# A retention layer and a low-rank mixer on one core: the prologue in another order

## The chip, the core and the metric

The kernel runs on one core of one Trainium2 chip. The metric is the time of one execution on the device in microseconds. The kernel before takes 223.32 us (median of 4 runs, 223.24 to 223.55). Engines are named as in the profile: PE is TensorE (PEld its weight loads), DVE is VectorE, ACT is ScalarE, POOL is GpSimd, SP is SyncE, which issues transfers.

## What is computed

The inputs q, k and v have 4 batches, 8 heads, 768 positions and 64 columns. A recurrent retention with one decay per head gives x with 512 columns per position; a low-rank mixing over positions (U: 768x32, V: 32x768) is added to x; an MLP (512 to 2048 and back, relu) is added to that.

```python
state = gamma * state + k_t outer v_t            # per batch and head, 64x64
y_t   = scale * q_t @ state
x     = y as [batch, 768, 512]
u     = x + (x^T @ U @ V)^T
out   = u + relu(u @ w_ch1) @ w_ch2
```

## The kernel before, in words

The recurrence is done in chunks: inside a chunk, scores of k against q are masked and multiplied with v; what came earlier enters as a state matrix. The decays are multiplied into q and k beforehand.

Batch 0 is the prologue. It is done in three blocks `sc` = 0, 1, 2 of 256 positions. For each block `prep_block` scales or casts the loaded halves of k, q and v (engine "P" is GpSimd, "D" VectorE, "A" ScalarE; `prep_pair` does both halves); `turn_block` transposes k or q on TensorE, with a copy from PSUM by the engines in its string; `score_block` makes scores of one parity and masks them (where its engine is "A", ScalarE copies to `a_raw` and GpSimd applies the mask); `state_half` adds half a block's outer products to the state bank and ScalarE copies the state; `mix_block` multiplies state by q and scores by v into two PSUM banks, which are copied to `xs[0]`. `keep_busy` issues matmuls whose result nobody reads. The loop at line 858 writes this out for all three blocks, one block's mix standing in the next block's round.

After the loop GpSimd casts w_ch1 (`prep_w1`), the last block is mixed, `spread_v` and `spread_u` lay V and U out with selection matmuls, `x_turn` transposes x into four PSUM banks, `lr_proj` multiplies x by U, line 909 adds V times that to the transposed x, and the copies of those banks are the input of batch 0's MLP (line 755).

From there on `weave` interleaves the MLP pieces of one batch with the attention of the next, at marks given as shares of the MLP's length. Each engine runs its instructions in program order. `prep_keys` scales k and q of batch 1 on GpSimd (line 306), `turn_pe` turns them on TensorE (line 465).

Loads are issued on SP's queue in one fixed list: batch 0's k, q, v by block, then U and V, w_ch1, the first four loads of batch 1, w_ch2, the rest of batch 1. Sixteen are issued at the start; after that `feed_one` issues one each time a loaded buffer has been taken, into a ring of 16 buffers. PSUM banks come from rings by tag; "mlp" is a ring of three.

Of the kernel before, what the change touches and what calls it, by code (L numbers as in the profile page):

```python
# [10 lines left out]
bf16 = mybir.dt.bfloat16  # L11
fp16 = mybir.dt.float16
AF = mybir.ActivationFunctionType
ALU = mybir.AluOpType
# [4 lines left out]
def kernel(  # L19
# [11 lines left out]
    nc = tc.nc  # L31
    P = 128
    B, H, S, D = q.shape
# [38 lines left out]
    def bank(tag, dtype=fp32):  # L72
        n_bank[0] += 1
        ring = RINGS[tag]
        ring.append(ring.pop(0))
        return psum.tile([P, 2048 // (4 if dtype == fp32 else 2)], dtype,
                         tag=f"bank{ring[-1]}", name=f"{tag}_{n_bank[0]}",
                         bufs=1)
# [4 lines left out]
    def evac(eng, dst, src):  # L83
        if eng == "A":
            nc.scalar.activation(dst, src, AF.Copy)  # L85
        else:
            nc.vector.tensor_copy(out=dst, in_=src)
# [49 lines left out]
    def feed_one(hold=True):  # L137
        if n_fed[0] == len(feed):
            return
        if hold and feed[n_fed[0]][0][:2] == ("k", 3):  # L140
            return
        key, src = feed[n_fed[0]]
        n_fed[0] += 1
        if key[0] == "uv":
            nc.sync.dma_start(
                out=Uf.rearrange("p s two r -> p s (two r)"),
                in_=moe_U.rearrange("(s p two) r -> p s (two r)", p=P, two=2))
            nc.sync.dma_start(
                out=Vf, in_=moe_V.rearrange("r (f t) -> (r f) t", f=NSC))
            return  # L150
        t = rin.tile([P, 512], fp32, tag="in", name=f"in_{n_fed[0]}")
        ready[key] = t
        if key[0] in "qkv":
            t = t.rearrange("p (h d) -> p h d", h=H if len(key) == 3 else 4)
        nc.sync.dma_start(out=t, in_=src)
# [28 lines left out]
    def keep_busy(n, fresh=False, wide=False):  # L184
        if fresh:
            idle_bank[0] = bank("mlp")
        if wide:
            for i in range(n):
                nc.tensor.matmul(idle_bank[0], ones[:, :P], ones, start=True,
                                 stop=True, skip_group_check=True)  # L190
            return
        for i in range(4 * n):
            nc.tensor.matmul(idle_bank[0][:, ts(i % 4, P)], ones[:, :P],  # L193
                             ones[:, :P], start=True, stop=True,
                             skip_group_check=True)
# [110 lines left out]
                nc.gpsimd.tensor_tensor(t, src, g, op=ALU.mult)  # L306
            feed_one()

    def prep_uv():
        take("uv")  # L310
        nc.gpsimd.tensor_copy(out=Uh, in_=Uf)
        nc.gpsimd.tensor_copy(out=Vh, in_=Vf)
        feed_one()

    def spread_u():
        u_p = bank("mlp")
# [6 lines left out]
        return u_p  # L323

    def hold_u(u_p):
        evac("A", Ub.rearrange("p (s x) r -> p x s r", x=2),
             u_p[:, :NCK * RK].rearrange("p (x s r) -> p x s r", x=2, s=NSC))

    def spread_v():
# [21 lines left out]
    live = {}  # L351
    n_state = [0]

    def turn_block(nm, sc, eng):
        src = pre[nm, sc]
        t = blk.tile([P, 4, 2, P], bf16, tag=nm + "T0",
                      name=f"{nm}T0_{sc}")
        np_ = 4 // len(eng)
        for g in range(len(eng)):
            tp = bank("mlp", bf16)  # L360
            for p in range(np_):
                for par in range(2):
                    nc.tensor.transpose(
                        tp[:, ds(2 * P * p, 2 * P)].rearrange(
                            "p (x two m) -> p two x m", x=2, two=2)[:, par],
                        src[:, par, ds(2 * (np_ * g + p), 2)], ident)
            o, i = (t[:, ds(np_ * g, np_)].rearrange("p n x m -> p (n x) m"),
                    tp[:, :2 * P * np_].rearrange("p (n m) -> p n m", m=P))
            if nm == "q":
                o = o.rearrange("p n (m two) -> p n two m", two=2)  # L370
                i = i.rearrange("p n (two m) -> p n two m", two=2)
            evac(eng[g], o, i)
        live[nm, sc] = t

    def state_half(sc, x):

        kd, vb = pre["k", sc], pre["v", sc]
        first = sc == 0 and x == 0
        if first:
            live["st_p"] = bank("st")  # L380
            live["st", 0, 0] = None
        st_p = live["st_p"]
        r = ds(HP * x, HP)
        for par in range(2):
            for p in range(4):
                nc.tensor.matmul(st_p[:, ts(p, P)], kd[r, par, ds(2 * p, 2)],  # L386
                                 vb[r, par, ds(2 * p, 2)],
                                 start=(first and par == 0 and p == 0),
                                 stop=True, skip_group_check=True)
        ns = states[n_state[0] % NST]  # L390
        n_state[0] += 1
        for i in range(2):
            ri = ds(D * i, D)
            evac("A", ns[ri, :, ri], four(st_p)[ri, :, ri])
        live["st", sc + x, 1 - x] = ns
# [22 lines left out]
                nc.gpsimd.tensor_tensor(a, t, m, op=ALU.mult)  # L418
            live["a", sc, par, i] = a

    def mix_block(sc, engs, tags=("o", "qk")):
        if sc == 0:
            xs[0] = xp.tile([P, NCK, DM], fp16, tag="x", name="x_0")
        qT, vb = live.pop(("q", sc)), pre["v", sc]
        o_p = [bank(t) for t in tags]
        for x in range(2):
            st = live.pop(("st", sc, x))
            if st is not None:
                for p in range(4):
                    nc.tensor.matmul(o_p[x][:, ts(p, P)], qT[:, p, x], st[:, p],  # L430
                                     start=(p == 0), stop=False,
                                     skip_group_check=True)
        for par in range(2):
            for h in range(H):
                for x in range(2):
                    r = ds(HP * x, HP)
                    nc.tensor.matmul(
                        o_p[x][:, ts(h, D)],
                        live["a", sc, par, h % 2][r, h // 2], vb[r, par, h],
                        start=(sc == 0 and x == 0 and par == 0 and h == 0),  # L440
                        stop=True, skip_group_check=True)
        for x in range(2):
            evac(engs[x], xs[0][:, 2 * sc + x], o_p[x])

    def turned(nm, b, sc):
        if (nm, b, sc) not in live:
# [90 lines left out]
        uTs[b] = xp.tile([P, NCK, NCB, P], fp16, tag="uT", bufs=1,  # L539
                         name=f"uT_{b}")  # L540

    def lr_proj(b):
        p_p = bank("o" if b else "s")
        for j in range(NCK):
            for c in range(NCB):
                nc.tensor.matmul(p_p[ds(RK * c, RK), :P], Ub[:, j],
                                 xs[b][:, j, ts(c, P)], start=(j == 0),
                                 stop=(j == NCK - 1))
        pcs[b] = rmid.tile([P, P], fp16, tag="pc", name=f"pc_{b}")
        evac("D", pcs[b], p_p[:, :P])  # L550

# [296 lines left out]
    def prep_pair(nm, sc, engs):  # L848
        for hh in range(2):
            prep_block(engs[hh], nm, sc, hh)  # L850
# [4 lines left out]
            nc.vector.tensor_scalar(u_sel[:, x, two], udiff,  # L855
                                    float(two - P * x), None, op0=ALU.is_equal)
    prep_pair("q", 0, "PD")
    for sc in range(NSC):
        last = sc + 1 == NSC
        keep_busy(3 if sc else 9, fresh=not last, wide=not sc)  # L860
        turn_block("k", sc, "D")
        keep_busy(0 if sc else 7, wide=True)
        turn_block("q", sc, "AD" if last else "A")
        prep_pair("v", sc, "PD" if last else "PA")
        if sc:
            state_half(sc - 1, 1)
        else:
            keep_busy(4)
        score_block(sc, 0)
        if last:  # L870
            prep_uv()
        else:
            prep_pair("k", sc + 1, "PD")
            prep_block("P", "q", sc + 1, 0)
            keep_busy(0 if sc else 3)
        if sc:
            score_block(sc, 1, "mlp", "DA")
        else:
            score_block(sc, 1)
        if last:  # L880
            u_p = spread_u()
            state_half(sc, 0)
            hold_u(u_p)
            mix_block(sc - 1, "AD")
            continue
        prep_block("D", "q", sc + 1, 1)
        if sc:
            mix_block(sc - 1, "AA")
        keep_busy(4 if sc else 1, fresh=sc > 0)
        state_half(sc, 0)  # L890
        if sc == 0:
            nc.vector.tensor_scalar(mask, jmat, srange, None, op0=ALU.is_ge)
    for mb in range(4):
        prep_w1(mb)
    mix_block(NSC - 1, "AD", ("s", "s"))
    spread_v()
    x_turn(0, 0)
    x_turn(0, 2)
    block_stack.close()
    gtp = ctx.enter_context(tc.tile_pool(name="gtp", bufs=1))  # L900
    outp = ctx.enter_context(tc.tile_pool(name="outp", bufs=6))
    lr_open(0)
    lr_proj(0)
    for c in range(1, NCB):
        x_turn(c, 0)
        x_turn(c, 2)
    idle_bank[0] = bank("s")
# [129 lines left out]
```

## Time and profile before

| what | value |
|---|---|
| median of 4 runs | 223.32 us |
| the profiled execution | 223.55 us, its span 221.8 us |
| TensorE busy | 213.4 us, 96% of the span |
| VectorE, ScalarE, GpSimd busy | 144.3, 91.2, 83.5 us |
| batch 0's MLP begins (first L755) | 28.13 us |
| batch 1's second q is turned (L465) | 57.42 and 58.42 us |
| read from HBM, written | 27.46 MB, 6.29 MB |

The profile is one execution; its times count from the start of the span. The page gives busy time per engine, 40 slices of the span, DMA queues, and the chain of work that ended last. Other views used are the timeline of one engine (start, length, engine, line, operation, in brackets the idle time before it and who ended it), the waits, and the chain in order of time. A row with x4 or x16 is that many instructions in a run. TensorE's matmuls overlap, so lengths of single rows add up to more than the time they take.

### The profile page before, as it was taken

To read this page: it belongs to the slowest core of one execution; us is meant where nothing else is said; L and a number is where in the kernel's file an instruction comes from. 1 tells how busy PE (TensorE), PEld (TensorE's weight loads), DVE (VectorE), ACT (ScalarE), POOL (GpSimd) and SP (SyncE) were. 2 spreads that over 40 slices of the span, in tenths; PEclk is the share of its full clock that TensorE was granted. 3 is DMA by queue.
4 is the path that set the end of the run, shared out by engine and by line. 5 is a ranking of instruction groups with operands and counts; after the bars stand their busy time and mean duration, and the time that the engine had idled before them with its cause. 6 is when DMAs were issued, how large, how long until landed. Compare 5 with 4: busy or idle time off the path is not lost.

```text
span 221.8 us, 5520 instructions
## 1 busy us (share of the span) xinstructions
PE 213.4 (96%) x2235; PEld 147.7 (67%) x2235; DVE 144.3 (65%) x306; ACT 91.2 (41%) x187; POOL 83.5 (38%) x121
## 2 busy tenths in 40 slices
PE   7879999999899999999999999999999999999994
PEld 2668854595455555666778884756788856668884
DVE  7578656225474567698897756498868542867543
ACT  3357654474556223775712005666420035551000
POOL 5467777887978868000099900000000000000000
PEclk9999999999999999999999999999999999999999
DMA  5998999999999999999999597900000961000043
GB/s 167 302 292 239 271 354 255 339 386 225 239 239 232 243 207 233 162 317 257 218 228 214 142 179 193 141 0 3 1 3 33 148 218 29 4 0 0 7 162 118
DMA packets 84489, 38.82 MB, mean 175 GB/s; under 512 B 58384, under 2 KB 77552, under 8 KB 84464
## 3 DMA queue, kind: packets, MB, share of 16 engines
q1 hardware_dynamic: 83456, 36.84, 71.4%
q10 hardware_dynamic: 1008, 1.64, 2.3%
q8 instruction: 17, 0.28, 0.6%
q14 instruction: 8, 0.07, 0.1%
HBM read 27.46 MB, written 6.29 MB: 152 GB/s over the span
## 4 chain that ended last, share of the span: by engine, by line
PE 66%; DMA 15%; DVE 10%; POOL 2%; ACT 2%; issue 2%; SPq 1%; DVEq 0%; ACTq 0%
PE mlp L755 26%; PE A L647 13%; DMA in<-in_moe_w_ch_dram 7%; PE C L647 6%; DMA in<-in_k_dram 6%; PE mlp L803 5%; PE B L647 3%; DVE a L512 3%; DMA in<-in_q_dram 2%; DVE gS L600 2%; PE s L506 2%; PE o L528 2%; ACT qT L85 2%; POOL qd L306 1%; PE mlp L193 1%
## 5 line engine op out<-in xcount | busy, mean ns | idle before, releaser
L755 PE MATMUL mlp<-uT,w1b 128*128 128x512 f16 (+1 forms) x512 | 88.7, 326 | 0.2 <-DVE gT L760 0.2
L762 ACT ACTIVATE gT<-mlp 128x512 f16<-128x512 f32 (+1 forms) x94 | 45.3, 490 | 59.3 <-PE mlp L755 57.1
L755 PEld LDWEIGHTS <-w1b 128*128 128x128 f16 x512 | 48.3, 98 | 31.1 <-issue 0.5
L760 DVE TENSOR_SCALAR gT<-mlp 128x512 f16<-128x512 f32 (+1 forms) x34 | 18.9, 556 | 27.9 <-PE mlp L755 27.5
L647 PEld LDWEIGHTS <-gT 128*128 128x128 f16 x288 | 27.6, 98 | 3.5
L512 DVE TENSOR_TENSOR a<-s,mask 128x512 bf16<-128x512 f32 x36 | 23.1, 683 | 10.0 <-PE s L506 9.9
L803 PE MATMUL mlp<-w2b,gT 128*128 128x512 f16 x96 | 24.4, 380 | 0.0
L85 ACT ACTIVATE x<-o 128x512 f16<-128x512 f32 x20 | 11.9, 596 | 23.9 <-PE o L528 23.8
L306 POOL TENSOR_TENSOR kd<-in,gk 128x512 bf16<-128x512 f32 x18 | 19.3, 1080 | 4.7 <-DMA in<-in_k_dram 4.7
L647 PEld LDWEIGHTS <-gS 128*128 128x128 f16 x200 | 19.3, 98 | 2.6
L306 POOL TENSOR_TENSOR qd<-in,gq 128x512 bf16<-128x512 f32 x18 | 19.3, 1089 | 0.0
L647 PE MATMUL A<-w2t,gT 128*128 128x256 f16 x144 | 18.2, 273 | 0.0
L85 ACT ACTIVATE state<-st 64x256 bf16<-64x256 f32 x40 | 15.0, 375 | 5.4 <-PE st L386 3.3
L304 POOL CAST vd<-in 128x512 bf16<-128x512 f32 x18 | 11.8, 666 | 2.4 <-DMA in<-in_v_dram 1.9
L803 PEld LDWEIGHTS <-gT 128*128 128x128 f16 x96 | 8.1, 98 | 6.9
L340 POOL CAST w1b<-in 128x512 f16<-128x512 f32 x16 | 9.7, 617 | 3.2 <-DMA in<-in_moe_w_ch_dram 2.6
L346 POOL CAST w2b<-in 128x512 f16<-128x512 f32 x16 | 9.7, 617 | 1.7 <-DMA in<-in_moe_w_ch_dram 1.1
L647 PE MATMUL B<-w2b,gT 128*128 128x256 f16 x72 | 9.3, 273 | 0.0
L647 PE MATMUL A<-w2t,gS 128*128 128x256 f16 x72 | 9.2, 273 | 0.0
L647 PE MATMUL A<-w2b,gT 128*128 128x256 f16 x72 | 9.0, 273 | 0.0
L565 DVE TENSOR_TENSOR x<-s,x 128x256 f16<-128x256 f32 (+1 forms) x16 | 8.1, 550 | 1.3 <-issue 0.7
L600 POOL COPY gate<-gT 128x1 f16<-128x1 f16 x1 | 0.2, 191 | 22.7 <-DVE gT L760 22.7
(147 smaller groups left out, 281.4 us busy)
## 6 DMA issues: line engine op xcount, KB each, us to landing
in<-in_moe_w_ch_dram SPq DMA_DIRECT2D x32, 256.0 KB, 5.5
in<-in_k_dram SPq DMA_DIRECT2D x24, 256.0 KB, 5.4
in<-in_q_dram SPq DMA_DIRECT2D x24, 256.0 KB, 4.6
in<-in_v_dram SPq DMA_DIRECT2D x24, 256.0 KB, 5.3
out_dram<-o SPq DMA_DIRECT2D x16, 256.0 KB, 2.2
out_dram<-o ACTq DMA_DIRECT2D x6, 256.0 KB, 2.5
out_dram<-o SPq DMA_DIRECT2D x3, 128.0 KB, 1.7
Uf<-in_moe_U_dram SPq DMA_DIRECT2D x1, 96.0 KB, 5.9
```

The costliest lines, as they stand in the source:

```text
L85: nc.scalar.activation(dst, src, AF.Copy)
L304: nc.gpsimd.tensor_copy(out=t, in_=src)
L306: nc.gpsimd.tensor_tensor(t, src, g, op=ALU.mult)
L340: nc.gpsimd.tensor_copy(out=w1b[:, c, ts(mb, 512)], in_=take("w1", mb, c))
L346: nc.gpsimd.tensor_copy(out=w2b[:, m], in_=take("w2", m))
L512: nc.vector.tensor_tensor(a, four(sp[i]), causal(mask), op=ALU.mult)
L565: nc.vector.tensor_tensor(us[b][:, ds(j0, nj), ts(c, P)], four(grown[b][c])[:, :nj], xs[b][:, ds(j0, nj), ts(c, P)], op=ALU.add)
L647: nc.tensor.matmul(acc[key, i], lhs[:, m, ts(i, P)], rhs[:, m], start=(fresh and m == 0), stop=(m == NH - 1), skip_group_check=True)
L755: nc.tensor.matmul(g_p[:, :sz], w1b[:, c, ts(m, P)], uTs[b][:, ds(j, nj), c], start=(c == 0), stop=(c == NCB - 1))
L760: nc.vector.tensor_relu(gT[:, m, ds(lo, sz)], g_p[:, :sz])
L762: nc.scalar.activation(gT[:, m, ds(lo, sz)], g_p[:, :sz], AF.Relu)
L803: nc.tensor.matmul(ch, gT[:, m, ts(j, P)], w2b[:, m], start=(m == 0), stop=(m == NM - 1))
```

## The change

The loop over the blocks is written out and its steps stand in another order.

- Block 2's k is prepared by GpSimd alone (before: GpSimd and VectorE), block 2's v likewise.
- In block 1's round, block 0's mix, the turn of block 2's k and the state of block 1's first half stand together; the two runs of filler matmuls that stood after block 0's mix and ahead of block 2's k turn are gone. GpSimd's half of block 2's q comes after its second score mask.
- Block 1's mix stands ahead of the turn of block 2's q. `mix_block` is split for that (open, state, near, out); the state of block 1's second half stands between the two halves of q's turn. The copies of the mix's two banks are ScalarE's, before and after block 2's second scores.
- `prep_uv` becomes `prep_u` and `prep_v`; U's spread follows block 2's first state, V's cast stands after block 2's mask on GpSimd. U's copy `hold_u` goes from ScalarE to VectorE, ahead of the last x copies.
- Two of the four x turns stand ahead of V's spread and of `lr_proj`, instead of one.

```diff
-    def prep_uv():
+    def prep_u():
         take("uv")
         nc.gpsimd.tensor_copy(out=Uh, in_=Uf)
+        feed_one()
+
+    def prep_v():
         nc.gpsimd.tensor_copy(out=Vh, in_=Vf)
-        feed_one()
...
     def hold_u(u_p):
-        evac("A", Ub.rearrange("p (s x) r -> p x s r", x=2),
+        evac("D", Ub.rearrange("p (s x) r -> p x s r", x=2),
...
-    def turn_block(nm, sc, eng):
+    def turn_block(nm, sc, eng, gs=None):
...
+    def mix_block(sc, engs):
+        mix_open(sc)
         for x in range(2):
-            evac(engs[x], xs[0][:, 2 * sc + x], o_p[x])
+            mix_state(sc, x)
+        mix_near(sc)
+        for x in range(2):
+            mix_out(sc, x, engs[x])
...
+    keep_busy(3, fresh=True)
+    turn_block("k", 1, "D")
+    turn_block("q", 1, "A")
+    prep_pair("v", 1, "PA")
+    state_half(0, 1)
+    score_block(1, 0)
+    prep_pair("k", 2, "PP")
+    score_block(1, 1, "mlp", "DA")
+    prep_block("P", "q", 2, 0)
+    mix_block(0, "AA")
+    turn_block("k", 2, "D")
+    state_half(1, 0)
+    prep_block("D", "q", 2, 1)
+
+    mix_open(1)
+    mix_state(1, 0)
+    mix_near(1)
+    mix_state(1, 1)
+    turn_block("q", 2, "AD", 0)
+    state_half(1, 1)
+    turn_block("q", 2, "AD", 1)
+    prep_pair("v", 2, "PP")
+    prep_u()
+    mix_out(1, 0, "A")
+    score_block(2, 0)
+    score_block(2, 1, "mlp", "DA")
+    mix_out(1, 1, "A")
+    state_half(2, 0)
+    u_p = spread_u()
+    prep_v()
     for mb in range(4):
         prep_w1(mb)
-    mix_block(NSC - 1, "AD", ("s", "s"))
-    spread_v()
+    mix_open(2, ("s", "s"))
+    mix_state(2, 0)
+    mix_near(2)
+    mix_state(2, 1)
+    hold_u(u_p)
+    mix_out(2, 0, "A")
+    mix_out(2, 1, "D")
     x_turn(0, 0)
     x_turn(0, 2)
+    x_turn(1, 0)
+    x_turn(1, 2)
+    spread_v()
...
     lr_open(0)
     lr_proj(0)
-    for c in range(1, NCB):
+    for c in range(2, NCB):
         x_turn(c, 0)
         x_turn(c, 2)
```

`lr_proj` also gets an argument for a part of its chunks, which the changed kernel doesn't use.

## The prediction

> **What bounds the kernel now.** I read the page first, then the chain of waits in order of time, then the timelines of TensorE and GpSimd. Parts 1 and 4 of the page:
>
> ```profile
> PE 213.4 (96%) x2235; PEld 147.7 (67%) x2235; DVE 144.3 (65%) x306; ACT 91.2 (41%) x187; POOL 83.5 (38%) x121
> ...
> PE 66%; DMA 15%; DVE 10%; POOL 2%; ACT 2%; issue 2%; SPq 1%; DVEq 0%; ACTq 0%
> ```
>
> TensorE looks like the bound, but 15% of the chain is DMA, and the chain in order of time shows where (start, length, what):
>
> ```profile
> 23.48 7.37 DMA in<-in_moe_w_ch_dram
> ...
> 30.91 6.15 DMA in<-in_k_dram
> ...
> 48.00 6.96 DMA in<-in_k_dram
> ...
> 58.42 0.52 PE qk L465 x6
> ```
>
> From 23.48 to 58.42 us nothing that TensorE does is on the chain: it runs from transfer to transfer, through batch 1's k and q. The TensorE timeline (start, length, engine, line, in brackets the idle time before and who ended it) says the same from the other side:
>
> ```profile
> 28.13 1.10 PE L755 MATMUL mlp<-uT,w1b 128*128 128x512 f16 x4
> ...
> 57.42 0.28 PE L465 MATMUL qk<-ident,qd 128*128 128x128 bf16 x2
> 58.42 0.51 PE L465 MATMUL qk<-ident,qd 128*128 128x128 bf16 x6 [0.72 <-POOL qd L306]
> ...
> 60.35 0.38 PE L465 MATMUL qk<-ident,kd 128*128 128x128 bf16 x4
> ```
>
> Batch 0's MLP begins at 28.13 and TensorE has no gap until 57.7. There it stands 0.72 us for a q that GpSimd scales, and a last matmul begun at 59.85 (0.22 us to the next) is followed by k's turn only at 60.35: 0.28 us more. GpSimd's rows give the cause of both:
>
> ```profile
> 55.03 1.08 POOL L306 TENSOR_TENSOR kd<-in,gk 128x512 bf16<-128x512 f32 x1 [0.44 <-DMA in<-in_k_dram]
> 56.08 2.29 POOL L306 TENSOR_TENSOR qd<-in,gq 128x512 bf16<-128x512 f32 x2
> ...
> 59.26 1.04 POOL L306 TENSOR_TENSOR kd<-in,gk 128x512 bf16<-128x512 f32 x1 [0.34 <-DMA in<-in_k_dram]
> ```
>
> GpSimd waits for k's landing at 54.96 (then kd, two qd: 58.37, TensorE starts 58.42), and for the next k at 59.19 (kd done 60.31, TensorE 60.35). So the prologue has about 0.72 + 0.28 = 1.0 us of slack against the load stream. After 60.35 the order of all engines is as before.
>
> **Does the change move the load stream?** The order of the loads on SP's queue is the same in both kernels. In the trace no load from the first w1 block to batch 1's k at 59.19 waits for its buffer: the block issued at 25.62, for instance, takes the buffer of block 2's second k half (zero-based), released at 18.10, now about 17.3; the last w1 block, issued at 30.25, takes v's second half, released at 21.76, now 21.4. What holds the issues is the landing of the load eight places before (issue 30.25 after landing 30.19, 30.91 after 30.85, 31.60 after 31.54) or the queue itself. So a prologue that takes its data earlier or somewhat later starts no load at another time.
>
> **The change part by part**, in the profiled execution's times.
>
> 1. *Block 2's second k half goes from VectorE to GpSimd.* GpSimd was idle from 16.22 to 18.27. The half landed at 15.89, so at the 1.04 us of GpSimd's own row it lies 16.22 to 17.26; VectorE did it 17.42 to 18.10. The third mask of block 1 on VectorE moves up by 0.6 us.
>
> 2. *GpSimd's mask ahead of block 2's first q half.* a_raw is there at 17.47. The two rows of this operation:
>
> ```profile
> 19.27 1.61 POOL L418 TENSOR_TENSOR a<-a_raw,mask 128x512 bf16<-128x512 bf16 x1
> ...
> 22.84 1.16 POOL L418 TENSOR_TENSOR a<-a_raw,mask 128x512 bf16<-128x512 bf16 x1 [0.54 <-ACT a_raw L85]
> ```
>
> It ends at 18.66 or 19.1; I take the first, since the 1.61 ran beside VectorE's q, which now lies elsewhere. The q half behind it ends at 19.70 (or 20.15); before, 19.31. This is a cost: 0.39 us (to 0.84) on what waits for it, the turn of q.
>
> 3. *28 filler matmuls go* (rows of 1.07 and 0.84 us, of which about 1.8 us stood in TensorE's way), and block 2's k turn (0.44) and the state of block 1's first half (0.55) take their place: 17.31 to 18.30. Block 1's mix follows, waits for the GpSimd mask and ends at 19.1 to 19.5 instead of 23.9. It was 1.1 us of TensorE between block 2's scores and block 2's mix.
>
> 4. *Block 2's q and scores.* TensorE turns the first q half at 19.75; ScalarE copies it 20.15 to 20.9 (0.75); the state (0.55) and the second half go between; VectorE copies 20.95 to 21.67 (0.72); the scores' first round ends at 21.9. Before it was 21.86: nothing gained, up to 0.45 lost.
>
> 5. *Masks and mix of block 2.* VectorE's three masks (0.65 each) end at 23.9 (before 23.73). ScalarE has state, one x, a_raw, x, state: a_raw at 22.3 to 22.9, the last state at 24.25 (before 23.71). GpSimd takes v's second half too (0.61, behind it U), then the mask, 22.95 to 24.1, then V (0.40), so w1's casts begin at 24.5 instead of 23.95. The mix ends at 24.75; before, it began at 23.95 and ended at 25.13.
>
> 6. *x turned ahead.* Two turns (0.45) to 25.2, V's spread (0.35) to 25.55, while x is copied; the projection (0.45) to 26.0; two turns to 26.45; V's copies on ScalarE end at 26.6. The product at line 909 starts at 26.65 instead of 27.06, and its copies and filler take the same 1.07 us: MLP at 27.7. Shortest ends everywhere give 27.25, longest 28.2. U's copy (0.33) goes to VectorE under the mix's wait.
>
> Cover of w1's later casts: the fourth is done at 26.8 and is needed at 27.7; without these 0.9 us, the first MLP tile would wait for it one for one. From the fifth on GpSimd waits for landings (26.33, 27.58, 28.22, 30.19), as before.
>
> Sum at the MLP: -0.43 us (from -0.9 to +0.1). Sum at 58.42 and 60.35: the wait grows from 1.0 to 1.4 us and everything after stands. On the span 221.8 us: 0.0. The profiled execution took 223.55 us, 1.75 around its span; the median is 223.32. Forecast 223.3 us.
>
> **Two rules weighed against rows.** The page's clock row is 9 in all 40 slices: full clock, which prices the loss of the filler at 0. The Trainium skill (TensorE: Matmul & The Clock Gate, Part 1) speaks against the change: an idle window of about 3.4 us halves the clock, and it takes about as long busy to return. An estimate from it: 3.4 us of matmul at half speed lose 1.7 us; less the slack of 1.0 and the 0.4 gained, +0.3 us in the end. I take 0: in the walk above TensorE stands for at most some 1.2 us at a time, near 23 us.
>
> The second speaks on the stream. The page has
>
> ```profile
> q8 instruction: 17, 0.28, 0.6%
> ```
>
> 16 KB packets on the same DMA engines. One at 15.05 us lasted 1.2 us and the landings around it are 2.2 us apart instead of 0.9; one at 63.86 put a k 2.1 us behind its neighbour instead of 1.15. The skill (Runtime: NRT & Kernel Launch, Instruction fetch mechanics) says that 256 instructions come as such a block, at a cost mostly hidden. By the rule the change costs 0 here; by the rows, a block costs the stream up to 1.3 us. The new kernel has 56 TensorE instructions fewer ahead of the MLP, so later blocks are asked for about 28 matmuls further on: the one at 51.73 comes near 52.7, the one at 33.38 near 36. The same five blocks fall before the landings of 56.84 and 59.19, so I take 0, with both ends of about -0.6 and +0.9 us.
>
> VectorE and ScalarE gain or lose nothing else: no operation of theirs is added, and the ring of three PSUM banks stands one step further at batch 1, where the copy it then waits for ended at 85.17 and the bank is written at 85.46.
>
> **Rivals.**
> - *The stream comes later (slower).* The block near 52.7 us falls among k and q transfers; if it costs 0.95 us there, as the one at 63.86 did, instead of the small delay seen at 51.73, qd and kd end up to 0.9 us later: 223.8 to 224.3. It decides from a landing 0.45 us later than 59.19. For: rows above. Against: as many blocks as before.
> - *The prologue is late past its cover (slower).* MLP after 29.1: GpSimd's two added casts (1.65 us) wholly exposed, or the clock. 223.8 to 224.5.
> - *The gain passes through (faster).* If SP's issues do follow the prologue, or GpSimd's chain at 55 us begins earlier, 0.4 to 0.9 us arrive: 222.4 to 222.9. Against: GpSimd's waits for landings.
> - *The stream comes earlier (faster)*, by 0.5 us or so: 222.8.
> - *The change does nothing at the MLP*: long ends in 2 and 4, 28.1; the same time as the forecast.
>
> **How the numbers follow.** Forecast with the last rival 0.52; stream later 0.17; prologue past cover 0.06; gain through 0.14; stream earlier 0.11. About 0.2% (0.45 us) is what a measurement of this kernel can tell: faster 0.25, same 0.52, slower 0.23. The likeliest case alone spans 222.9 to 223.75. Of the outer cases the middle parts belong in the range: 222.4 to 224.2.
>
> **What would show it.** Right: the first L755 at 27.3 to 28.1; the idle before the six L465 matmuls on qd near 1.1 us instead of 0.72; kd at 59.3; L465 on kd still at about 60.35. Wrong in step 2: GpSimd's q half after 20.2. Wrong on the stream: k landing away from 54.96 and 59.19 by over 0.4 us. Wrong in the core: TensorE past 60.35 earlier, with the landings where they were; or a clock row below 9 between 17 and 30 us.

## The result, and the profile after

The changed kernel takes 224.03 us (median of 35 executions, 222.83 to 226.85) against 223.18 us for the kernel before on the same chip (56 executions). The ratio is 1.0034, with a 95% interval of 1.0020 to 1.0048: about 0.76 us slower. The forecast was 223.3 us. The profiled execution of the changed kernel took 224.48 us, its span 222.7 us. Parts 1 and 4 of its page:

```profile
PE 212.9 (96%) x2207; PEld 146.5 (66%) x2207; DVE 145.0 (65%) x304; ACT 91.2 (41%) x187; POOL 84.1 (38%) x123
...
PE 69%; DMA 14%; DVE 8%; POOL 3%; ACT 2%; issue 2%; SPq 0%; DVEq 0%
```

TensorE does 0.5 us less and the span is 0.9 us longer. The chain in order of time (start, length, what):

```profile
23.00 7.06 DMA in<-in_moe_w_ch_dram
...
48.06 7.90 DMA in<-in_k_dram
56.03 1.04 POOL kd L306
57.08 2.19 POOL qd L306 x2
59.31 0.52 PE qk L484 x6
59.86 1.35 ACT qO L85 x2
61.25 0.38 PE qk L484 x4
```

The chain still runs from transfer to transfer, and TensorE joins it at 59.31 instead of 58.42. The row after it corrects the reading of the prediction: k's turn at 61.25 (60.35 before) follows ScalarE's two copies of q. It comes 1.92 to 1.94 us behind q's turn in all 20 traces of this study, and does not wait for k's own landing. The TensorE timeline (start, length, engine, line, operation, in brackets the idle time before and who ended it):

```profile
22.19 0.31 PE L407 MATMUL s<-qT,kT 64*64 64x128 bf16 x8 [0.56 <-DVE qT L87]
...
28.23 1.10 PE L778 MATMUL mlp<-uT,w1b 128*128 128x512 f16 x4
...
58.31 0.28 PE L484 MATMUL qk<-ident,qd 128*128 128x128 bf16 x2 [0.64 <-POOL qd L306]
59.31 0.51 PE L484 MATMUL qk<-ident,qd 128*128 128x128 bf16 x6 [0.72 <-POOL qd L306]
```

The MLP begins at 28.23, not at 27.7, and TensorE waits for q twice. GpSimd in the prologue, then VectorE, in the same columns:

```profile
15.47 2.04 POOL L276 TENSOR_TENSOR k<-in,gk 128x512 bf16<-128x512 f32 x2 [0.97 <-DMA in<-in_k_dram]
17.81 1.15 POOL L421 TENSOR_TENSOR a<-a_raw,mask 128x512 bf16<-128x512 bf16 x1 [0.30 <-ACT a_raw L85]
18.93 1.04 POOL L276 TENSOR_TENSOR q<-in,gq 128x512 bf16<-128x512 f32 x1
...
23.53 1.16 POOL L421 TENSOR_TENSOR a<-a_raw,mask 128x512 bf16<-128x512 bf16 x1 [1.54 <-ACT a_raw L85]
```

```profile
19.47 1.05 DVE L276 TENSOR_TENSOR q<-in,gq 128x512 bf16<-128x512 f32 x1 [0.49 <-DMA in<-in_q_dram]
21.41 0.73 DVE L87 COPY qT<-mlp 128x512 bf16<-128x512 bf16 x1 [0.89 <-PE mlp L367]
```

VectorE's half of block 2's q (zero-based) takes 1.05 us here. In the kernel before the same row was shorter, since GpSimd's half (18.27 to 19.31) was nearly over when it began:

```profile
19.13 0.73 DVE L276 TENSOR_TENSOR q<-in,gq 128x512 bf16<-128x512 f32 x1 [0.43 <-DMA in<-in_q_dram]
```

One trace is one execution, so a second one of the changed kernel was taken later (g1_after_again, profiled execution 224.53 us). The marks of the three, in us; "first scores" are TensorE's first s matmuls of the block, "q" and "k" the turns at lines 465 and 484:

| | first scores, block 0 | block 1 | block 2 | MLP | q's second turn | k's turn | MLP of batch 1 | end |
|---|---|---|---|---|---|---|---|---|
| before | 9.63 | 15.77 | 21.21 | 28.13 | 58.42 | 60.35 | 84.28 | 221.77 |
| after | 9.89 | 16.04 | 21.32 | 28.23 | 59.31 | 61.25 | 85.22 | 222.71 |
| after, second trace | 9.71 | 15.86 | 21.14 | 28.05 | 58.70 | 60.63 | 85.28 | 222.75 |

From block 0's first scores to the MLP the new order takes 18.34 us in both its traces, 18.50 before. The prologue is not where these two executions lose. What follows the start of batch 1's MLP is not either: it takes 137.5 us in all 20 traces. The loss lies between, in two waits.

The first is for q. TensorE needs 29.3 to 29.4 us from the MLP's start to q's second turn when nothing stops it (this is so in 12 of the 20 traces). It is 30.29 us before, and 31.09 and 30.65 us here, because q comes late.

The second lies between k's turn and batch 1's MLP. The shortest of the 20 traces needs 23.47 us for it (e3); it is 23.93 us before, and 23.97 and 24.65 us here. So the first trace loses 0.80 us to q; the second loses 0.36 us to q and 0.72 us to this later wait. VectorE's sums of w2 blocks (`w2t`, line 600, now 623) meet GpSimd's k there. VectorE and GpSimd before, then in the second trace:

```profile
68.62 0.41 DVE L600 TENSOR_TENSOR w2t<-w2b,w2t 128x512 f16<-128x512 f16 x1
68.84 2.09 POOL L306 TENSOR_TENSOR kd<-in,gk 128x512 bf16<-128x512 f32 x2 [0.50 <-DMA in<-in_k_dram]
```

```profile
68.71 2.23 POOL L306 TENSOR_TENSOR kd<-in,gk 128x512 bf16<-128x512 f32 x2 [0.70 <-PE s L525]
68.95 1.08 DVE L623 TENSOR_TENSOR w2t<-w2b,w2t 128x512 f16<-128x512 f16 x1
```

Begun 0.22 us ahead of GpSimd, the sum takes 0.41 us; begun 0.24 us behind it, 1.08 us. The masks that TensorE waits for follow it on VectorE. This sum's delay is all of the stretch's excess: in each of the 20 traces its start beyond 7.81 us behind k's turn, with its length beyond 0.41 us, makes up within 0.02 us what the stretch takes beyond 23.47 us. The excess is 0 to 1.2 us, with a mean of 0.4 us in either order.

### The profile page after: what moved, and what is told of

Read it like the earlier page. It is cut to its first block, busy times and chain, and to the rows that moved or that the text cites. A ratio compares the mean times of both kernels' runs of the same rounds, so it can differ in the third digit from the quotient of the medians.

```text
span 222.7 us, 5462 instructions
## 1 busy us (share of the span) xinstructions
PE 212.9 (96%) x2207; PEld 146.5 (66%) x2207; DVE 145.0 (65%) x304; ACT 91.2 (41%) x187; POOL 84.1 (38%) x123
## 4 chain that ended last, share of the span: by engine, by line
PE 69%; DMA 14%; DVE 8%; POOL 3%; ACT 2%; issue 2%; SPq 0%; DVEq 0%
PE mlp L778 26%; PE A L670 13%; DMA in<-in_moe_w_ch_dram 7%; DMA in<-in_k_dram 7%; PE C L670 6%; PE mlp L826 6%; PE B L670 3%; PE mlp L189 3%; DVE a L531 2%; DVE gS L623 2%; PE s L525 2%; PE o L547 2%; POOL qd L306 1%; PE mlp L367 1%; PE o L542 1%
```

## The experiments

Every execution also lists its mean granted TensorE clock. For the kernel before it was 0.998 or more in all 312 executions beside the experiments. For the changed kernel it was 0.991 or 0.992 in 11 of 36, with a median of 224.76 us against 223.69 us for the other 25. That splits the loss: by means, +0.83 us in all; +0.51 us (0.24 to 0.80) in the executions at full clock alone; so about 0.3 us is clock, and 0.5 us is something else. "At full clock" means 0.995 or more from here on. An execution without a clock record is listed at 1.0 too: four of the 20 profiles (after, e6, e7, f3) have no clock row. At that share, an estimate from these counts, some five of the 25 would have no record and one or two of them a low clock unseen, which is worth less than 0.1 of the 0.5 us. All kernels below do the whole computation; the edits move work or add and remove fillers.

### The clock: fillers taken from the old order, and given to the new one

e3_old_no_fill takes the 28 fillers of block 1's and 2's rounds out of the kernel before and puts 27 more matmuls at the start:

```diff
-        keep_busy(3 if sc else 9, fresh=not last, wide=not sc)
+        keep_busy((9, 3, 0)[sc], fresh=not last)
...
-        keep_busy(4 if sc else 1, fresh=sc > 0)
+        keep_busy(0 if sc else 1)
```

> The kernel before without the 28 fillers, and with the start's nine wide ones as 36 narrow, so that the instruction count is kept. Theory 1: 223.0 to 223.3, no slower than before. Theory 2: slower by 0.3 to 1 us, with a mean clock of 0.992 in a part of the executions.

Measured: 224.32 us, ratio 1.0067 (1.0038 to 1.0097). In 6 of 12 executions the clock was 0.983 to 0.985 (median 225.37 us); the other six have a median of 223.33 us. So the old order loses its clock too when its fillers go. It is not the other start: e5, below, has the same start with all its fillers, and none of 22 executions below 0.995.

e4_new_filled gives the changed kernel fillers in the waits of both mixes:

```diff
     mix_state(1, 0)
+    idle_bank[0] = bank("s")
+    keep_busy(3)
...
     turn_block("q", 2, "AD", 1)
+    keep_busy(1)
...
     mix_state(2, 0)
+    idle_bank[0] = bank("o")
+    keep_busy(3)
```

> The changed kernel with 28 narrow fillers put back where TensorE waits: 12 ahead of block 1's near mix, 4 after block 2's second q turn, 12 ahead of block 2's near mix. Count and filler are both restored. Theory 1 and theory 2 both say about 223.2 to 223.4; theory 2 says that no execution shows a clock under 1.0. If it stays at 224.0, neither is the cause.

Measured: 223.20 us, ratio 1.0011 (0.9997 to 1.0026), no execution of 22 below 0.995. It was run again beside another kernel:

> The same kernel as e4_new_filled (the changed kernel with fillers in both waits), again, beside the next one on one chip. If its 223.20 was right: 223.0 to 223.4, no execution below 0.995. If the 223.85 of its sister with one k half on VectorE tells more of the filled order: 223.6 to 223.9.

Measured: 223.27 us, ratio 1.0001 (0.9983 to 1.0018), again none of 22. Two kernels have fillers in one of the two waits, and 15 more narrow matmuls at the start, which were to leave the instruction count as it was:

```diff
-    keep_busy(9, fresh=True, wide=True)
+    keep_busy(5, fresh=True)
+    keep_busy(4, wide=True)
```

> The changed kernel with 12 narrow fillers in the wait of block 1's near mix only (instruction count kept at the kernel before's by 20 narrow for 5 wide fillers at the start). Clock theory: if the weak stretch lies near 19 us, no execution shows 0.992 and the median is 223.2 to 223.5; if it lies near 24 us, a fifth to a third still do and the median is 223.6 to 223.9.

> The changed kernel with 12 narrow fillers in the wait of block 2's near mix only, count kept in the same way. Clock theory: the other way round; no 0.992 and 223.2 to 223.5 if the weak stretch lies near 24 us, else 223.6 to 223.9. If both of these two lose the low clock, either stretch alone is enough to keep the window busy.

Measured: e7 (block 1's mix) 223.91 us, 1.0032 (1.0017 to 1.0047), none of 22 below 0.995; e8 (block 2's mix) 223.88 us, 1.0018 (1.0000 to 1.0036), 1 of 22. Over all kernels of the new order, those with fillers in the wait of either mix have 1 of 176 executions below 0.995, those with none 23 of 93 (after 11 of 36, its repeat 7 of 22, e1 below 4 of 21, f1 below 1 of 14). So the clock part of the loss is shown: the fillers hold the clock, and the change removed them. What no run shows is where the clock falls: no profile that was kept shows a lowered clock in the prologue. A clock of 0.992 over 222 us is 1.8 us of lost clock, and e3's 0.984 is twice that. TensorE's busy time in two stretches of 3.4 us, for the kernel before and then after (the stretch and its length; PE, PEld, DVE, ACT, POOL with their instructions; granted clock; DMA share; GB/s):

```profile
14.00:17.40 3.40, 2.56 (x86) 2.13 (x84) 2.09 (x4) 2.95 (x6) 1.27 (x2) 1.00 1.17 295
20.80:24.20 3.40, 3.28 (x95) 2.63 (x92) 2.96 (x7) 2.89 (x8) 2.86 (x6) 1.00 0.71 231
```

```profile
14.00:17.40 3.40, 2.55 (x88) 2.18 (x85) 2.08 (x5) 2.68 (x5) 2.43 (x3) 1.00 1.17 294
20.80:24.20 3.40, 2.82 (x72) 2.05 (x68) 2.40 (x4) 2.99 (x7) 1.81 (x4) 1.00 0.88 277
```

The first profile of the changed kernel has no clock record, so the 1.00 in its rows stands for none. In the second stretch TensorE falls from 96% busy to 83% (second trace: 2.70 us, 79%), with no idle time longer than 0.6 us. But a busy share does not tell when the clock falls: the first stretch is at 75% in both kernels, with 0.85 us idle at a time, and the kernel before kept its clock. e7 is busy for 2.57 of 3.40 us from 22.30 us on, and kept it too.

### Does the instruction count, by the blocks of instructions, move the time?

The prediction gave the 56 TensorE instructions fewer, and with them the place of the 16 KB instruction blocks in the stream, two ends of -0.6 and +0.9 us. e1 restores the changed kernel's count at the start, e5 adds the same to the kernel before, e2 and e6 take instructions away by making narrow fillers wide (one 512-column matmul for four of 128 columns):

```diff
-    keep_busy(9, fresh=True, wide=True)
+    keep_busy(9, fresh=True)
```

> The changed kernel, with the nine wide filler matmuls at the very start written as 36 narrow ones (the same columns, 27 instructions more), so that TensorE's instruction count ahead of the MLP is again within one matmul of the kernel before. Theory 1 (the blocks of TensorE's instructions are fetched about 28 matmuls later and one of them now falls on batch 1's second k): the k lands near 55.0 us again instead of 55.96, qd ends near 58.4, the time goes back to 223.2 to 223.5. Theory 2 (the missing filler lets the clock fall in some executions): nothing changes, about 224.0, and about a third of the executions show a mean clock of 0.992. If both act: about 223.6.

> The kernel before with the nine wide fillers at the very start as 36 narrow ones: 54 TensorE instructions more ahead of everything, the same columns. Theory 1 (where the instruction block falls in the load stream sets when batch 1's second q is scaled): the block comes about 27 matmuls earlier, before w2's last load has landed; k lands 3.5 us behind that load or less (3.51 before, 4.47 in the changed kernel) and the time is 222.8 to 223.1. Rival (the block's place does not matter, the stream only varies from execution to execution): 223.1 as before, and k anywhere.

> The kernel before with its 28 narrow fillers after block 0's mix and ahead of block 2's k turn as 7 wide ones, and the 12 ahead of the MLP as 3 wide ones: the same filler time, 60 TensorE instructions fewer (the change has 56 fewer). Theory 1: slower by 0.4 to 0.8 us, 223.6 to 224.0, k landing near 56.0, with the clock at 1.0. Theory 2: as before, 223.2, since the filler is all there.

> The kernel before with every narrow filler of the prologue as a wide one: 126 TensorE instructions fewer, the same columns. Theory 1: the block that came at 51.73 comes after batch 1's second k has landed, so k is no later than 3.5 us behind w2's last load, and the delay falls on what follows; 222.8 to 223.4. Rival: 223.1 as before.

Measured: e1 223.73 us, 1.0030 (1.0014 to 1.0046), 4 of 21 with low clock, +0.29 us (0.04 to 0.54) at full clock; e5 223.55, 1.0009 (0.9989 to 1.0028); e2 223.28, 1.0018 (1.0000 to 1.0037); e6 224.18, 1.0024 (1.0002 to 1.0046), 2 of 22 with low clock. As a theory of the loss this did not come out: neither sign of the count gives a gain, and the losses of e1 and e2 at full clock, 0.3 us each, barely leave 0. e6's loss has a reason of its own: wide fillers all through the prologue put the MLP 18.95 us behind the first scores (18.50 before).

The traces did show what a block does where it falls. In the kernels with more narrow matmuls at the start, the block that is asked for at 14.4 to 15.5 us elsewhere comes at 12.6 to 13.7, ahead of block 2's k. Its first half lands at 14.77 to 15.73 us elsewhere (after 15.31, f3 15.25), but at 16.02 in e1, 16.07 in e7, 16.68 in e8, 16.62 in e3 and 15.88 in g2 (below). Of the six kernels with such a start only e5, whose block comes first, at 12.58, has it at 15.63. GpSimd's series k, k, mask, q starts from it in the new order, and in e1, e7 and e8 VectorE's q then lies beside GpSimd's for its whole length. GpSimd and VectorE of e1:

```profile
16.18 2.04 POOL L276 TENSOR_TENSOR k<-in,gk 128x512 bf16<-128x512 f32 x2 [1.80 <-DMA in<-in_k_dram]
18.18 1.15 POOL L421 TENSOR_TENSOR a<-a_raw,mask 128x512 bf16<-128x512 bf16 x1
19.29 1.04 POOL L276 TENSOR_TENSOR q<-in,gq 128x512 bf16<-128x512 f32 x1
```

```profile
19.32 1.56 DVE L276 TENSOR_TENSOR q<-in,gq 128x512 bf16<-128x512 f32 x1
```

VectorE's q takes 1.56 us instead of 0.73. By the chain it is not what holds e1: that runs from k's landing over GpSimd's k to the turn of k, which TensorE waits for. From block 1's to block 2's first scores it is 5.76 us in e1 and 5.28 in both traces of the changed kernel; with fillers, 6.61 in e7 and 6.36 in e8, but 5.92 in e4 and f3, which have none added at the start. So e7 and e8 do not test the clock alone: each carries its own late k.

### Is there 1.0 us of slack ahead of the stream?

e11 puts three more wide fillers, 0.65 us, ahead of the MLP in the kernel before:

```diff
     keep_busy(3)
+    keep_busy(3, wide=True)
```

> The kernel before with three more wide fillers (0.65 us of TensorE) right ahead of the MLP: it measures the slack itself. The prediction's claim (1.0 us of slack against the load stream): no change, 223.2. The theory after the first runs (in most executions the loads are early and TensorE arrives without a wait): slower by 0.3 to 0.65 us, 223.5 to 223.9.

Measured: 223.56 us, 1.0016 (1.0000 to 1.0033), +0.44 us (0.17 to 0.71) by means. With 1.0 us of slack it would have been nothing. The traces say why. The same load, w2's last, lands anywhere from 47.7 to 52.4 us in the 20 traces, with the same list of loads; in the three kernels that have two traces each, it lands 0.2, 0.9 and 1.3 us apart. TensorE waits 0.7 us for q in six of them (before, after twice, e2, e3, e10), where that load lands at 51.2 us or later, 0.3 us in two, and not at all in twelve; the changed kernel filled (e4) is one:

```profile
58.44 0.61 PE L484 MATMUL qk<-ident,qd 128*128 128x128 bf16 x8
```

Of the eight traces of the old order, TensorE waits for q in four (before, e2, e3, e10) and not at all in the other four (e5, e6, e11, f2). So the wait of the prediction's profile is not there each time, and where it is missing there is no slack and the prologue sets the time.

### GpSimd's series k, k, mask, q

e10 gives the kernel before the same load on GpSimd, k's second half and the mask ahead of q's first half, and leaves its order else:

```diff
-            prep_pair("k", sc + 1, "PD")
-            prep_block("P", "q", sc + 1, 0)
+            prep_pair("k", sc + 1, "PP" if sc else "PD")
+            if not sc:
+                prep_block("P", "q", sc + 1, 0)
...
             score_block(sc, 1, "mlp", "DA")
+            if not last:
+                prep_block("P", "q", sc + 1, 0)
```

> The kernel before with one part of the change alone: both halves of block 2's k on GpSimd, and GpSimd's half of block 2's q behind its mask. GpSimd theory: block 2's scores 0.5 to 1.2 us later than before (12.0 to 12.7 us after block 0's first, 11.5 before), VectorE's q half stretched over 1.0 us where it runs beside GpSimd's, and slower by 0.3 to 0.8 us: 223.5 to 224.0, with a full clock. Rival (stream alone, or the missing filler alone): 223.2 as before.

Measured: 223.26 us, 1.0008 (0.9990 to 1.0026). The expectation of a loss is missed: by its trace the stretch between block 1's and block 2's first scores is 5.43 us (5.44 before). In the old order the k turn and fillers lie behind and cover it.

e12 takes k's second half back to VectorE in the filled new kernel, and was repeated beside f3:

```diff
-    prep_pair("k", 2, "PP")
+    prep_pair("k", 2, "PD")
```

> The changed kernel with its 28 fillers in the waits, and with block 2's second k half back on VectorE: one part undone. GpSimd theory: GpSimd reaches the mask up to 1 us earlier where k lands late, and nothing where the mask waits for ScalarE's copy anyway; 222.9 to 223.2. Rival: 223.2 as with both on GpSimd.

> The same kernel as e12_new_k_on_dve (the filled kernel with block 2's second k half on VectorE again), again, beside the one before on one chip. If the difference of 0.65 us between the two was real, 223.7 to 223.95 and above the one before by 0.4 us or more; if it lay in the chip or the hour, within 0.25 us of it.

Measured: 223.85 us, 1.0032 (1.0020 to 1.0045), and 223.91 us, 1.0031 (1.0015 to 1.0047); 0.64 us above its sister f3 on the same chip. The expectation of e12 is missed: the k half on VectorE costs time. The difference is real and the traces show it. TensorE, VectorE, GpSimd of f4:

```profile
18.03 0.40 PE L367 MATMUL mlp<-ident,k 128*128 128x128 bf16 x4
18.95 0.40 PE L367 MATMUL mlp<-ident,k 128*128 128x128 bf16 x4 [0.52 <-DVE k L276]
```

```profile
18.21 0.68 DVE L276 TENSOR_TENSOR k<-in,gk 128x512 bf16<-128x512 f32 x1
18.81 0.68 DVE L416 TENSOR_TENSOR a<-mlp,mask 128x512 bf16<-128x512 f32 x1
19.41 0.68 DVE L87 COPY kT<-mlp 128x1024 bf16<-128x1024 bf16 x1
20.01 1.45 DVE L276 TENSOR_TENSOR q<-in,gq 128x512 bf16<-128x512 f32 x1
```

```profile
18.32 1.58 POOL L421 TENSOR_TENSOR a<-a_raw,mask 128x512 bf16<-128x512 bf16 x1 [1.40 <-ACT a_raw L85]
```

The new order turns block 2's k right behind block 0's mix, so VectorE's k, behind two masks, is waited for (0.52 us; with both halves on GpSimd, f3 turns all eight at 17.43 without a gap), and VectorE's k and q meet GpSimd's mask and q, which costs either side a wait: the mask 1.58 instead of 1.15, q 1.45 instead of 0.68. From block 1's to block 2's first scores it is 6.51 us against 5.92 in f3. So the k half on GpSimd is what this order needs, and no cause of the loss.

e9 (filled) and f1 (not filled) give block 1's GpSimd mask to VectorE in the new order, f2 does so in the old one:

```diff
-    score_block(1, 1, "mlp", "DA")
+    score_block(1, 1, "mlp", "DD")
```

> The changed kernel with its 28 fillers in the waits, and with block 1's second masks both on VectorE, so that no mask stands on GpSimd between block 2's k and q. GpSimd theory (two k halves, a mask and a q half in one row on GpSimd hold block 2's scores): from the first score matmul of block 0 to block 2's first about 11.4 us or less instead of 11.9 to 12.7, the first MLP matmul 18.4 to 18.9 us after block 0's first scores instead of 19.4, and 222.7 to 223.1 us, no slower than before. Rival (the load stream alone decides, as the prediction had it): the same 223.2 as with the mask on GpSimd.

> The changed kernel with block 1's second mask of the ScalarE/GpSimd parity given to VectorE ('DD' for 'DA' in that score block), so that GpSimd goes from block 2's k straight to its first q half; no filler is added. Theory A (0.3 us of the loss is the clock, the rest is GpSimd's series k, k, mask, q): some 2 to 5 of 20 executions still show a mean clock below 0.995, and those at full clock lie at 223.1 to 223.4, no longer at 223.7. Theory B (the rest is the load stream that meets instruction blocks elsewhere): the full-clock ones stay at 223.6 to 223.9. Theory C (in the earlier run of this mask with fillers, 222.90, the fillers did it all): the same as B.

> The kernel before with the same mask given to VectorE in block 1's round alone. Control for the run beside it: if that mask on GpSimd is a price of the new order, 223.0 to 223.4 here, no difference from the kernel before. If the mask's place is worth as much in either order, 222.7 to 222.9, and then it explains nothing of the difference between the orders.

Measured: e9 222.90 us, 1.0000 (0.9983 to 1.0016), none of 22 below 0.995; f1 223.29 us, 1.0012 (0.9989 to 1.0035), 1 of 14 below, +0.13 us (-0.14 to 0.41) at full clock; f2 223.41 us, 0.9994 (0.9971 to 1.0018). GpSimd and VectorE of f1:

```profile
16.32 2.04 POOL L276 TENSOR_TENSOR k<-in,gk 128x512 bf16<-128x512 f32 x2 [2.13 <-PE st L389]
18.32 1.04 POOL L276 TENSOR_TENSOR q<-in,gq 128x512 bf16<-128x512 f32 x1
```

```profile
20.47 0.68 DVE L276 TENSOR_TENSOR q<-in,gq 128x512 bf16<-128x512 f32 x1
```

GpSimd's q ends at 19.36, before VectorE's begins, which keeps its 0.68 us; the stretch to block 2's first scores is 5.00 us instead of 5.28. The rest of the loss falls from about 0.5 to 0.13 us, as expected of the series, and the old order gains nothing from the same edit. But the intervals (0.24 to 0.80, and -0.14 to 0.41) overlap: this points to the mask in GpSimd's series, and does not show it.

### The changed kernel again, and the best of the parts

> The changed kernel as it is, for a second trace and more executions beside the kernel before on one chip. Theory A (series on GpSimd, stream as it falls): full-clock executions 223.5 to 223.8 again, 2 to 8 of 20 below 0.995; the stretch from block 1's first to block 2's first scores 5.3 to 5.8 us, longer with VectorE's q half (1.05 to 1.56 us); batch 1's k may land anywhere from 53 to 56 us. Theory B (this order meets instruction blocks so that the stream is late each time): batch 1's k lands at 55.7 or later again and TensorE stands for q by about 0.7 us at 58 to 59, as in the first trace.

Measured: 223.88 us, 1.0037 (1.0018 to 1.0056), 7 of 22 executions below 0.995, +0.46 us (0.08 to 0.85) at full clock. The loss and its split are confirmed. In the trace, TensorE:

```profile
57.70 0.28 PE L484 MATMUL qk<-ident,qd 128*128 128x128 bf16 x2 [0.20 <-POOL qd L306]
58.70 0.51 PE L484 MATMUL qk<-ident,qd 128*128 128x128 bf16 x6 [0.72 <-POOL qd L306]
```

TensorE again stands for q, as the stream theory has it, but k lands at 55.35 us, short of the 55.7 that it asked for. That k, the third load behind w2's last, lands 3.51 us behind it in the kernel before, 4.47 and 3.68 us in the two traces after. The instruction block near there was asked for 0.28, 1.23 and 0.57 us behind that load's landing; where no block falls between the two (e6, e8) it is 2.50 and 2.49 us. f1, with a block late between the two, has 3.30. So a block costs this k 0.8 to 2 us according to where it falls. That the new order meets it worse each time is not shown by two traces, and e1, which moves the block, has a shift of its own in the prologue.

g2 is the sum of what helped: the mask on VectorE, and fillers in block 2's mix wait alone, with e8's start:

```diff
-    keep_busy(9, fresh=True, wide=True)
+    keep_busy(5, fresh=True)
+    keep_busy(4, wide=True)
...
-    score_block(1, 1, "mlp", "DA")
+    score_block(1, 1, "mlp", "DD")
...
     mix_state(2, 0)
+    idle_bank[0] = bank("o")
+    keep_busy(3)
```

> The candidate for a better version: the changed kernel with the mask of block 1 on VectorE (as f1) and fillers in block 2's mix wait alone (as e8), 27 more narrow matmuls at the start less those in the wait so that the count stays. If the parts add up: 0 or 1 of 20 executions below 0.995, and 222.8 to 223.2, at or a little below the kernel before. If the stream or the start bounds the rest whatever the prologue does: 223.1 to 223.4.

Measured: 223.51 us, 1.0007 (0.9987 to 1.0027), none of 22 below 0.995. It doesn't beat the kernel before, and neither does e9.

### All of them against the length of the prologue

The stretch from block 1's first scores to the MLP in the trace, and the time at full clock against the kernel before on the same chip, by means, with 95% intervals:

| kernel | stretch, us | difference, us |
|---|---|---|
| f1, g2 (new, mask on VectorE) | 11.84, 11.84 | +0.13 (-0.14 to 0.41), +0.17 (-0.17 to 0.49) |
| after, again | 12.18, 12.19 | +0.51 (0.24 to 0.80), +0.46 (0.08 to 0.85) |
| f2, e5, e10 (old order) | 12.32, 12.32, 12.40 | +0.09, +0.19, +0.22 (all include 0) |
| before | 12.36 | 0 |
| e3, e2 (old, other fillers) | 12.38, 12.52 | +0.22 (0.00 to 0.44), +0.32 (0.02 to 0.64) |
| e9, e4, f3 (new, filled) | 12.52, 12.70, 12.70 | -0.10, +0.12, +0.08 (all include 0) |
| e1 | 12.67 | +0.29 (0.04 to 0.54) |
| e6, e11 (old) | 12.84, 12.91 | +0.71 (0.28 to 1.13), +0.44 (0.17 to 0.71) |
| f4, e12, e8, e7 | 13.27, 13.27, 13.27, 13.51 | +0.72, +0.67, +0.32, +0.63 (none includes 0) |

Half a microsecond less than the old stretch brings nothing; half a microsecond more arrives. That is the picture of a prologue and a stream that end together. The changed kernel stands off it most, by about 0.4 us.

## Why the prediction was wrong

Two terms of the sum were put at 0 and are not: the price of the lost fillers, and all that lies behind the MLP's start ("everything after stands", 0.0 on the span). The first measures about 0.3 us and its cause is shown. The second measures about 0.5 us at full clock. Its cause stays open; the two traces show it as 0.80 us of waiting for q, and as 0.36 us of that with 0.72 us of VectorE's sums waiting for GpSimd.

**The core** ("about 1.0 us of slack against the load stream") failed too. It was read off one execution in which TensorE waited for q. Of the 1.0 us, 0.28 was never the stream's: k's turn follows ScalarE's q copies by the chain. The other 0.72 is there in 6 of 20 traces. e11 shows that delays arrive. What holds of it is the other direction: f1 and g2 shorten the stretch by 0.5 us and gain nothing. It is not what makes the changed kernel slower, since its prologue is no longer.

**The clock rule, priced at 0,** has the best settled part of the loss: some 0.3 us. The prediction set it aside because TensorE never stands for long. The Trainium skill (TensorE: Matmul & The Clock Gate, Part 1) speaks of idle windows of about 3.4 us; here no idle time of TensorE from the first scores to the MLP is longer than 0.85 us, and that one is in the kernel before too, and yet 18 of 58 executions of the changed kernel lose clock. The estimate from that rule was +0.3 us: the right size by luck, since the sum was another, and the forecast left the clock to a rival with a chance of 0.06. The clock costs 1.1 to 1.2 us (224.76 against 223.69, 224.75 against 223.54) in three executions of ten, not 1.7 us once less a slack.

**Step 1** (k's second half on GpSimd, free) held: 16.47 to 17.52 us; e12 and f4 price the other choice at 0.64 us.

**Step 2** held: q's half ended at 19.97 us, 19.70 forecast, of which 0.26 is the first scores' later start in that execution.

**Step 3** held in its order: the k turn and state stood at 17.52 to 18.62, and block 1's mix ended at 19.92 (19.5 at the latest was forecast), just ahead of the turn of q.

**Step 4** was mis-sized, in TensorE's own series. The chain of the changed kernel (start, length, what) runs:

```profile
18.93 1.05 POOL q L276
20.02 0.40 PE mlp L367 x4
20.42 0.55 PE st L389 x8
20.97 0.34 PE mlp L367 x4
21.41 0.74 DVE qT L87
22.19 0.35 PE s L407 x8
```

Turn, state, second turn, copy and the rest of the scores stand one behind the other: 2.52 us from 20.02 to 22.54, where the forecast had 2.15 (19.75 to 21.9). The copy of the second half began at 21.41, 20.95 forecast (21.21 with the later start).

VectorE's q half was mis-sized as well, but off the chain: it ended at 20.52, before TensorE came to the second turn (20.90). It was taken as done in time at the 0.73 of its old row. It met GpSimd's, which the mask had pushed back, and took 1.05 (1.03 in the second trace, 1.56 at worst in e1). In each of these traces it ends 0.55 us behind GpSimd's half: 19.31 and 19.86 before, 19.97 and 20.52 after, 20.33 and 20.88 in e1, 20.91 and 21.46 in f4. So it waits for GpSimd's operation and does not share with it. The Trainium skill says just this (SBUF — State Buffer, section SBUF: two separate sides): a VectorE operation with two SBUF inputs and a GpSimd one that reads SBUF lock each other out for a whole instruction, and the one that starts first goes on. By that rule the step's own GpSimd half, ended at 19.70, gives VectorE 20.25; the prediction had both rows and did not put them together.

**Steps 5 and 6** follow from it: GpSimd's mask ended at 24.69, 24.1 forecast, and the MLP began at 28.23, 27.7 forecast. Of these 0.53 us, 0.26 is the start; the 0.27 left is about what remains of the 0.37 us by which the series in step 4 was too short. Against the first scores the gain is 0.16 us, not 0.43.

**The load stream.** The order of the loads and the waits of SP were as said, and w2's last load lands where it did (51.49, 51.45 before). The block of instructions came to 52.72 us, as worked out; it was priced at 0 with an upper end of +0.9, and in the profiled pair it is +0.9: q's second turn at 59.31 against 58.42. In the second trace the block comes at 52.24 and q's second turn at 58.70. This is the mechanism of the rival "the stream comes later", which gave 223.8 to 224.3. That this range holds the measured time is in part luck, since 0.3 us of the loss is the clock. Whether the stream is the rest of the loss over all executions stays open, see below.

**What would have shown it**: not the profile's clock row. It is 9 in all 40 slices of the changed kernel's second profile, since that execution is not among those that lost clock, and the first has no such row. The list of clocks per execution shows what that row can't.

**Open.** Of some 0.8 us (by means), 0.3 is the clock. The other 0.5 us is there at full clock, in both sets of executions, though the prologue is no longer by either trace. Without the mask on GpSimd it is 0.13 us, with e4's fillers 0.1, which a late stream alone would not explain. A larger share of executions with a late block, or with VectorE's sums begun behind GpSimd's k, would fit: both are in the traces. With two traces of the changed kernel and one of the kernel before, no run here tells them apart, or shows that the new order meets either more often.

## What to carry to other kernels

A wait for data in one profile is slack only if it is there in other executions too: look at how far the same load's landing scatters before pricing a gain or a loss at nothing. Matmuls that compute nothing may be holding the clock; before they are dropped, look at the granted clock of many executions, not at one profile's row. When an elementwise operation moves to another engine, look at what two-operand work of its neighbour it then meets, add the wait, and see whether the chain passes through it.

## What the runs showed of the hardware that was not expected

- The granted clock fell in about three of ten executions of the changed kernel, whose longest idle time of TensorE in the prologue is 0.85 us, as in the kernel before, which never lost clock; it fell in half of those of e3. 12 narrow fillers in one wait held it but for 1 of 66 executions (e7, e8, g2).
- Work with two SBUF operands on VectorE and GpSimd does not overlap: whichever starts first keeps its time, and the other's row is longer by its wait. VectorE's q reads 0.68 to 1.56 us by this, GpSimd's mask 1.15 to 1.61, and in f3, where VectorE's q began 0.03 us earlier, GpSimd's took 1.55 instead of 1.04 us. One such meeting, decided by 0.2 us, is worth 0.67 us of the whole kernel's time in the second trace.
- One 16 KB block of instructions among 256 KB loads puts the next landings 0.8 to 2 us later: 2.5 us for three loads without a block, 3.3 to 4.5 with it. The Trainium skill (Runtime: NRT & Kernel Launch, Instruction fetch mechanics) calls the cost mostly hidden. For TensorE, which asks for it, it is: the first profile of the changed kernel has no idle time at the blocks of 29.62, 36.26 and 52.72 us. For the loads it is not.
- The same load lands up to 4.7 us apart (47.7 to 52.4) in kernels with the same list of loads, and up to 1.3 us apart in two executions of one kernel.
